# Gating w_in on the first batch's strided queries, one head of band v ahead of all, a w_out quarter moved forward and a new plan, in a fused sparse-attention and feed-forward kernel

## The chip, the cores and the metric

One core of one Trainium2 chip. The metric is the device time of one execution in microseconds (us), as the median of several runs. Most executions of one kernel lie within 0.3 to 1% of each other. Beside each experiment the kernel before was run again on the same chip. A ratio is the mean time of one kernel's fast runs over the mean of the other's fast runs of the same rounds, with a 95% interval, so it is not quite the ratio of the medians that are quoted.

## The reference

Eight batches of eight heads, 576 tokens, head size 64. Heads 0 to 3 ("local") see the last 32 positions, heads 4 to 7 ("strided") every 32nd. The result is laid out as 4608 tokens of 512 and goes through a feed-forward layer.

```python
rel = pos[:, None] - pos[None, :]
mask_local   = (rel >= 0) & (rel < 32)
mask_strided = (rel >= 0) & (pos[None, :] % 32 == pos[:, None] % 32)
attn = softmax(where(mask, q @ k.T / sqrt(64), -1e9)) @ v
x = attn.transpose(0, 2, 1, 3).reshape(4608, 512)
h = relu(x @ w_in)               # w_in  512 x 2048
out = (s * h * h + b) @ w_out    # w_out 2048 x 512
```

## The kernel before

The program is not written in the order in which it runs. A small planner, `Plan`, holds a clock `t` for TensorE, a time `free` for each other engine, and for each piece of work the time at which the plan believes it done. It puts out TensorE's steps one by one, and each posted job goes to the engine that the plan believes to be free first. The result is one fixed order for each engine, and each engine works through its own list in order. If the plan's times are wrong, nothing computes wrongly, as semaphores guard the data, but an engine stands at a job whose data are not there while later jobs could run.

```python
class Plan:
    LAT = {"A": 70.0, "V": 70.0, "P": 70.0, "D": 9000.0, "X": 9000.0}   # ns until a result counts as there
    ...
    def flush(self):
        ...  # of the posted jobs that are ready, the one ready first
            eng = min(p[1], key=lambda e: max(self.free[e], r) + p[1][e])
            end = max(self.free[eng], r) + p[1][eng]
            self.free[eng] = end
            p[2](eng)                       # emits the instructions, on that engine
            for k in p[3]:
                self.done[k] = end + self.LAT[eng]
...
def landing(cost):                          # when the plan believes a load to land
    nonlocal ring
    ring = max(ring, plan.t + 2000.0) + cost
    return ring + (6000.0 if plan.t > 60000.0 else 0.0)
```

("A" is ScalarE, "V" VectorE, "P" GpSimd, "D" a DMA transpose of q or k, "X" a DMA transpose of x, both issued by SyncE.) From batch 4 on, k comes transposed by DMA, and so does q. q is then spread into a block form by a copy that may go to three engines:

```python
plan.post([("in", "k" + sfx, b, mm), ("s", (b - back, m), 2)], {"D": 1300.0}, k_dma, [("k", id_)])
...
plan.post([("qT", id_), ("s", (b - 1, m), 2)], {"P": 2000.0, "V": 940.0, "A": 1340.0}, q_spread, [("q", id_)])
```

All loads from DRAM in the steady state are issued by GpSimd. The fetch of batch b+2 is held back twice: by the plan, which posts it when k of batch b+1 counts as transposed, and on the chip by a one-element "gate" copy that reads the transposed k.

```python
def fetch_qk(b):
    for mm in range(2):
        if (b - 1, "kTs", mm) in loaded:
            nc.gpsimd.tensor_copy(out=gate[0:1, 2 + mm:3 + mm], in_=loaded[b - 1, "kTs", mm][0:1, 0, 0:1])
    load_qk(b)
    ...
plan.post([...] + [("q", (b, mk)) for mk in range(4)] + [("k", (b, mk)) for mk in range(4)] +
          [("k", (b + 1 if b > 1 else b, mk)) for mk in range(2, 4)],
          {"P": 0.0}, lambda eng, b=b: fetch_qk(b + 2), [("fetch", b + 2)])
```

The start: w_in waits, by such a gate, for band v (v of the local heads, staged in w_out's buffer), and w_out comes after q, k of the second batch.

```python
def weights_in(eng):
    nc.gpsimd.tensor_copy(out=gate[0:64, 2:4].bitcast(FP32), in_=vl_stage[64:128, 0, 0, 0:1])
    load_w_in(True)
...
def second(eng):
    fetch_qk(1)
    weights_out(range(4))
    load_vl(1)
```

The softmax here doesn't subtract the row's maximum and nothing guards it: scores larger than these inputs give would overflow.

## Time and profile before

| | before |
|---|---|
| time, median of 5 runs beside the changed kernel | 321.53 us (319.93 to 321.97) |
| span of the profiled run | 321.0 us (this run took 322.85 us, more than all five) |
| TensorE busy | 309.6 us, 96% |
| granted TensorE clock, mean | 0.997 |

TensorE is the bound almost everywhere, so the busy share says little. The document uses a ledger as the prediction does: **lag** is a time minus the TensorE work done until then, work being the count of matmuls by their back-to-back intervals. A lag that stays constant over a stretch says that nothing was lost in it. The lags from here on were taken from all traces by one program, whose sum of work is 298.0 us, 1.0 below the sum that the prediction made by hand, so they are to be compared with each other and not to a tenth with those of the prediction. Waits that the text gives without a view are counted in the same way, from start to start less the work, and come out 0.2 to 0.3 us longer than the idle time in brackets. In the kernel before: 16.8 us at the second batch's first weighted sum (51.7 us), 19.4 at batch 3's (97.2 us, after the stall at 88 to 92 us that the prediction shows), 18.9 at the end.

### The profile page before, as it was taken

How to read it: one execution, taken by the hardware profiler on the slowest of the kernel's cores; microseconds unless marked ns; L12 is line 12 of the kernel's file. 1: busy time of each engine (PE TensorE's matmuls, PEld its weight loads, DVE VectorE, ACT ScalarE, POOL GpSimd, SP SyncE). 2: the span in 40 equal slices, each digit the busy share in tenths (PEclk: the TensorE clock that was granted, in tenths of full speed). 3: DMA queues.
4: the chain of work that ended last, by engine and by line, in shares of the span. 5: the costliest groups of instructions: out<-in, count | busy, mean ns of one | idle time of the engine just before them, and what ended most of it. 6: DMA issues, size and time to landing. Idle time of an engine off the chain costs nothing.

```text
span 321.0 us, 5972 instructions
## 1 busy us (share of the span) xinstructions
PE 309.6 (96%) x2184; PEld 173.1 (54%) x2184; DVE 193.9 (60%) x539; ACT 160.7 (50%) x301; POOL 106.0 (33%) x151
## 2 busy tenths in 40 slices
PE   8987899999989999999999999999999999999994
PEld 3763555666646555555655465545654445544441
DVE  6665864788888779655877377745874124443211
ACT  3774953398855575057753363555652026643100
POOL 7291628840793039700972078300000000000000
PEclk9999999999999999999999999999999999999998
DMA  8999999999989869999999899997204310000121
GB/s 118 181 144 205 212 181 159 189 211 94 95 92 164 135 112 167 151 166 170 132 134 132 163 160 158 140 159 173 73 18 70 102 48 33 2 33 34 43 91 65
DMA packets 110944, 39.41 MB, mean 123 GB/s; under 512 B 94706, under 2 KB 104562, under 8 KB 110914
## 3 DMA queue, kind: packets, MB, share of 16 engines
q0 software_dynamic: 65776, 18.66, 66.2%
q1 hardware_dynamic: 45138, 20.37, 32.5%
q8 instruction: 17, 0.28, 0.4%
q14 instruction: 13, 0.11, 0.1%
HBM read 38.15 MB, written 10.91 MB: 153 GB/s over the span
## 4 chain that ended last, share of the span: by engine, by line
PE 83%; DMA 8%; ACT 4%; POOL 2%; issue 2%; DVE 1%; SPq 0%; POOLq 0%; ACTq 0%
PE ps_f L683 38%; PE ps_f L648 34%; DMA ql<-in_q_dram 5%; PE ps_a L542 4%; PE ps_s L490 4%; DMA w_out_sb<-in_v_dram 2%; PE ps_t L374 1%; PE ps_a L706 1%; ACT pt L504 1%; ACT qD_loc L303 1%; POOL w_in L290 1%; POOL v_loc L303 1%; PE ps_f L542 0%; ACT u L666 0%; DVE gT L672 0%
## 5 line engine op out<-in xcount | busy, mean ns | idle before, releaser
L683 PE MATMUL ps_f<-w_out_sb,gT 128*128 128x512 f16 x576 | 145.4, 379 | 1.3 <-DVE gT L672 1.3
L666 ACT ACTIVATE u<-ps_f 128x512 f16<-128x512 f32 x136 | 80.9, 597 | 89.1 <-PE ps_f L648 69.9
L648 PE MATMUL ps_f<-xT,w_in_sb 128*128 128x512 f16 x432 | 108.7, 379 | 2.1 <-DMA w_in_sb<-in_moe_w_in_dram 2.1
L672 DVE TENSOR_TENSOR gT<-u 128x512 f16<-128x512 f16 x144 | 59.7, 419 | 44.2 <-ACT u L666 43.3
L683 PEld LDWEIGHTS <-gT 128*128 128x128 f16 x576 | 54.5, 98 | 55.4 <-DVE gT L672 1.7
L648 PEld LDWEIGHTS <-w_in_sb 128*128 128x128 f16 x432 | 45.7, 114 | 36.3 <-DMA w_in_sb<-in_moe_w_in_dram 2.6
L504 ACT ACTIVATE pt<-ps_s 128x384 f16<-128x384 f32 (+2 forms) x96 | 43.7, 489 | 21.1 <-PE ps_s L490 20.1
L694 DVE SCALAR_TENSOR_TENSOR o<-ps_f,s_sb,bcs 128x512 f32<-128x512 f32 x36 | 26.9, 746 | 33.0 <-PE ps_f L683 32.8
L542 PEld LDWEIGHTS <-pt 72*72 72x72 f16 (+1 forms) x448 | 32.1, 119 | 17.2 <-issue 0.8
L568 DVE TENSOR_TENSOR x_nat<-ps_a,rec 72x256 f16<-72x256 f32 (+1 forms) x76 | 35.0, 461 | 1.7 <-DVE rec L557 0.3
L648 PE MATMUL ps_f<-xT,w_in 128*128 128x512 f16 x136 | 35.3, 379 | 0.1
L557 DVE RECIPROCAL rec<-ps_a 72x4 f32<-72x4 f32 (+1 forms) x76 | 13.8, 181 | 18.4 <-PE ps_a L542 18.0
L277 POOL DMA_DIRECT2D v_loc<-in_v_dram x28 | 24.2, 879 | 1.8 <-issue 0.6
L648 PEld LDWEIGHTS <-w_in 128*128 128x128 f16 x144 | 14.9, 114 | 9.9
L282 POOL DMA_DIRECT2D v_str<-in_v_dram x16 | 13.1, 819 | 11.9 <-PE ps_a L542 6.5
L738 POOL COPY gate<-kT 1x1 f16<-1x1 f16 x6 | 1.2, 194 | 47.4 <-DMA kT<-ks 47.4
L512 DVE TENSOR_TENSOR pt<-pt,mask_loc 128x384 f16<-128x384 f16 x42 | 14.1, 352 | 3.5 <-ACT pt L504 2.7
L542 PE MATMUL ps_a<-v_str,pt 72*72 72x65 f16 x204 | 15.3, 197 | 0.0
L512 DVE TENSOR_TENSOR pt<-pt,mask_str 72x432 f16<-72x432 f16 (+1 forms) x42 | 14.3, 348 | 1.6 <-ACT pt L504 1.0
L542 PE MATMUL ps_a<-v_loc,pt 128*96 128x65 f16 x150 | 12.3, 206 | 0.0
L252 POOL DMA_DIRECT2D ql<-in_q_dram x16 | 11.9, 754 | 0.9 <-issue 0.9
L490 PE MATMUL ps_s<-qD_loc,kT_loc 128*128 128x192 f16 x72 | 11.1, 246 | 0.6 <-ACT pt L504 0.3
(104 smaller groups left out, 251.4 us busy)
## 6 DMA issues: line engine op xcount, KB each, us to landing
out_dram<-o SPq DMA_DIRECT2D x36, 256.0 KB, 3.6
v_loc<-in_v_dram POOLq DMA_DIRECT2D x28, 80.0 KB, 9.6
w_out_sb<-in_moe_w_out_dram POOLq DMA_DIRECT2D x4, 512.0 KB, 12.4
qs<-in_q_dram POOLq DMA_DIRECT2D x6, 288.0 KB, 6.2
ks<-in_k_dram POOLq DMA_DIRECT2D x6, 288.0 KB, 7.8
x_dram<-x_nat SPq DMA_DIRECT2D x10, 144.0 KB
ql<-in_q_dram POOLq DMA_DIRECT2D x4, 288.0 KB, 7.2
kl<-in_k_dram POOLq DMA_DIRECT2D x4, 288.0 KB, 8.4
```

Of the source, the lines that this page charges most:

```text
L277: nc.gpsimd.dma_start(out=vl[:, h, 1:LT, 0:D], in_=rest[:, h])
L490: nc.tensor.matmul(out=st["s", g][0:nk, c:c + 2 * nq], lhsT=(st["k"][:, i * nq:i * nq + nk] if loc else st["k"][:, i, 0:SQ]), rhs=st["q"][ ...
L504: nc.scalar.activation(out=pt[0:nk, 0:2 * n].rearrange("k t c -> k (t c)"), in_=st["s", g][0:nk, 0:2 * n * nq], func=AF.Exp, scale=scale)
L512: nc.vector.tensor_tensor(out=pt[0:nk, 0:2 * n], in0=pt[0:nk, 0:2 * n], in1=mask, op=ALU.mult)
L542: nc.tensor.matmul(out=st["a"][0:nq, j % per, :], lhsT=st["pt", g][0:nk, i, :], rhs=vt[0:nk, 2 * mm + e, j, :])
L557: nc.vector.reciprocal(out=st["rec", e, j][0:nq, 0:per], in_=st["pa", e, j][0:nq, 0:per, D:D + 1])
L568: nc.vector.tensor_tensor(out=st["x"][:, j0:j0 + per, 64 * e:64 * e + 64], in0=st["pa", e, j][0:nq, 0:per, 0:D], in1=st["rec", e, j][0:nq, ...
L648: nc.tensor.matmul(out=gts["h", T, ft], lhsT=(w_in_sb[min(ft // 4, 2) - 1][:, ct, :] if ft > 3 else w_in0[ct]).rearrange("p (c x l) -> p c ...
L666: nc.scalar.activation(out=gts["u", T, ft], in_=gts["h", T, ft], func=AF.Relu)
L672: nc.vector.tensor_tensor(out=gts[T][:, ft, :], in0=u, in1=u, op=ALU.mult)
L683: nc.tensor.matmul(out=gts["o", T, ts], lhsT=gts[T][:, ft, ts * 128:(ts + 1) * 128], rhs=w_out_sb[:, ft, :], start=(ft == 0), stop=(ft == ...
L694: nc.vector.scalar_tensor_tensor(out=o, in0=gts["o", T, ts], scalar=s_sb[:, 0:1], in1=bcs, op0=ALU.mult, op1=ALU.add)
```

## The change

The intent is to shorten the start. w_in's loads wait for the strided queries of batch 0, which land earlier than band v, one head of band v is loaded ahead of everything, and a quarter of w_out goes ahead of the second batch's q. Local q and k of batch 0 are transposed head by head straight from the load. The plan's constants are then fitted anew, among them which batches use DMA transposes. Three of the new constants belong to the steady state: loads after 60 us count as landed 4 us late instead of 6, x transposes take 10 us instead of 9, and a new key, "soon", lets the plan post a fetch 3 us after k's transposes are queued rather than 9 us after, when they count as done.

```diff
-    LAT = {"A": 70.0, "V": 70.0, "P": 70.0, "D": 9000.0, "X": 9000.0}
+    LAT = {"A": 70.0, "V": 70.0, "P": 70.0, "D": 9000.0, "X": 10000.0}
...
-                self.done[k] = end + self.LAT[eng]
+                soon = isinstance(k, tuple) and k[0] == "soon"
+                self.done[k] = end + (3000.0 if soon else self.LAT[eng])
...
-    KB_DMA, QS_DMA, XS_DMA = 4, 4, 3
+    KB_DMA, QS_DMA, XS_DMA = 3, 3, 4
...
     nc.sync.dma_start(out=ident, in_=h_ident.ap())
+    stage_v(range(1))
...
-                      k_dma, [("k", id_)])
+                      k_dma, [("k", id_), ("soon", id_)])
...
-        return ring + (6000.0 if plan.t > 60000.0 else 0.0)
+        return ring + (4000.0 if plan.t > 60000.0 else 0.0)
...
+    nc.gpsimd.tensor_copy(out=gate[0:8, 2:3], in_=loaded[0, "qs"][64:SQ, 0:1])
+    load_w_in()
+    ring = 14400.0
...
     def second(eng):
+        weights_out(range(1))
         fetch_qk(1)
-        weights_out(range(4))
+        weights_out(range(1, 4))
...
-                        [("k", (b + 1 if b > 1 else b, mk)) for mk in range(2, 4)],
+                        [("soon" if b > 1 else "k", (b + 1 if b > 1 else b, mk)) for mk in range(2, 4)],
```

Cut here: w_in in three pieces instead of six, band v loaded head by head with its 32 overlapping rows copied on chip (`rows_before`, on ScalarE, VectorE or GpSimd), the head-by-head transposes of batch 0, and other planned costs and arrival times.

## The prediction

> **What bounds the kernel now.** I read the page first, then the chain of waits, the timeline of TensorE, and the landing times of single transfers. The busy row says TensorE, and the slices say that it is full everywhere but at the start:
>
> ```profile
> PE 309.6 (96%) x2184; PEld 173.1 (54%) x2184; DVE 193.9 (60%) x539; ACT 160.7 (50%) x301; POOL 106.0 (33%) x151
> PE   8987899999989999999999999999999999999994
> ```
>
> 96% flatters it: the first slices hold filler matmuls on a tile of ones (26 in the first 10 us), and a matmul's busy time covers its latency. So I used a ledger. Start-to-start intervals of back-to-back matmuls, off the timeline, are 0.216 us for a 512-column one, 0.042 and 0.032 for a transpose of 96 and 72 columns, 0.082 and 0.063 for a score, some 0.045 and 0.035 for a weighted sum over v. All matmuls of the program without the fillers, in these intervals, make 299.0 us. The last matmul ends at 317.0 us, so 18 us are filler and waiting; the last 4.0 us are an eviction and the last transfer. The **lag** (time minus work done) tells where the 18 us arose:
>
> - at 25.2 us (first 16 matmuls of the first projection, 512 columns each, done): work 12.9, lag 12.3
> - at 33.2 us (first transpose of the second batch's q): work 18.3, lag 14.9
> - at 51.7 us (second batch's first weighted sum): work 35.2, lag 16.5
> - at 65.5 us (third batch's): work 49.0, lag 16.5
> - at the end: lag 18.0
>
> From 51.7 us on only 1.5 us are lost, so what the change can win lies almost all in the first 50 us. There the chain that ended last shows a string of transfers:
>
> ```profile
> 1.27 4.38 DMA ql<-in_q_dram
> 5.67 0.73 SPq L772
> 6.45 7.25 DMA w_out_sb<-in_v_dram
> 14.30 1.33 POOL w_in L290 x3
> ...
> 18.38 0.72 POOL w_in_sb L292
> 19.10 0.72 POOL w_in_sb L293
> 19.82 12.51 DMA ql<-in_q_dram
> 32.35 0.84 ACT qp L303
> 33.24 0.44 PE ps_t L374 x6
> ```
>
> Columns: start, length, what. q of batch 0 lands, band v is staged (in the buffer that w_out fills later) until 13.7 us, only then GpSimd issues w_in, and second-batch q queues behind it until 32.3. The cost on TensorE, from its timeline:
>
> ```profile
> 25.21 3.62 PE L648 MATMUL ps_f<-xT,w_in_sb 128*128 128x512 f16 x16
> 30.97 2.13 PE L648 MATMUL ps_f<-xT,w_in_sb 128*128 128x512 f16 x9 [2.14 <-DMA w_in_sb<-in_moe_w_in_dram]
> 33.24 0.43 PE L374 MATMUL ps_t<-ident,qp 96*128 96x96 f16 x6
> ```
>
> A wait of 2.14 us for the last piece of w_in, then second-batch q. The landings: vs of batch 0 at 13.4, w_in at 18.1 to 20.7 (first quarter, four pieces), 24.8 and 30.9, then ql 32.3, kl 33.8, qs 35.7, ks 37.1, w_out 39.2, 41.7, 44.8, 46.7, band v 50.9. From 13.4 to about 15.8 us the software queue moves nothing: that hole is what the gate costs.
>
> **What the Trainium skill says.** "TensorE: Matmul & The Clock Gate", Back-to-back issue gap: a lone warm matmul takes N/2.4 + 2.5 ns, 215.8 ns for 512 columns, and N/1.2 cold. The trace agrees: 216 ns, and 0.427 us for each of the first fillers. "DMA: Bandwidth & Descriptors", Queues, rings and completion order: each DMA engine goes round robin between queues, a packet of descriptors at a time. The trace agrees only in part: the SyncE band-v loads were issued from 6.45 us, yet none of their packets starts before 10.5 us, when the software queue thins out. "SBUF — State Buffer", SBUF: two separate sides: VectorE and GpSimd share a port pair as an exclusive lock. The trace fits it: four VectorE casts of v, 0.90 us together at 13.5 us, take 2.58 us beside a GpSimd memset, and TensorE loses about 1.4 us there (0.97 us of it is in the row below):
>
> ```profile
> 88.01 2.58 DVE L303 COPY v_str<-vs 72x512 f16<-72x512 f16 x4
> 88.21 1.83 POOL L264 MEMSET qs<- 16x2048 f16 x1
> 91.25 0.39 PE L683 MATMUL ps_f<-w_out_sb,gT 128*128 128x512 f16 x1 [0.97 <-DVE gT L672]
> ```
>
> **The change, part by part.**
>
> Gate of w_in. It now hangs on the eight last rows of qs, issued at 3.40:
>
> ```profile
> L270 POOL DMA_DIRECT2D qs<-in_q_dram x2: 606/628/651, 2.8 to 3.4; - x2
> DMA to landing us min/median/max: 6.3/6.5/6.6
> ```
>
> 3.40 + 6.33 = 9.73 us, against 13.70 for v: 4.0 us earlier. Descriptors take 0.7 us an issue, so w_in stands behind ks and vs before they are through, and the hole is filled. The pieces took about 2.5, 4.1 and 6.1 us one after the other; with band v beside them I expect about 17.5, 20.5 and 26. The first 16 projections end by about 25, the next 16 take 3.46 us more (28.4), so the last piece is there in time and the **2.14 us wait goes**.
>
> Band v. One head (147 KB) goes ahead of everything, when the queues are empty. The 32 overlapping rows are copied on chip, so a batch needs 2304 descriptors instead of 2944. Cost: small copies on ACT, VectorE and GpSimd, all off the path, and a memset six times as long on VectorE (0.27 to about 1.6 us, done before q lands). Ql may land a few tenths later than 5.65.
>
> Batch 0's local q and k are transposed head by head. In the program's order this is 48 transposes for 24, the pairing copies (0.62 us VectorE, 0.82 GpSimd/ACT) gone. The 24 extra cost 24 × 0.042 = 1.0 us, in a stretch where TensorE ran fillers.
>
> Batch 3 moves to DMA transposes. 24 local transposes leave TensorE; the 16 strided q ones leave and 16 of x come back. Sum: **−1.0 us in the stage where TensorE is full**. The work total stays at 299.0: a microsecond has moved from the full stage into the idle one.
>
> w_out's first quarter ahead of second-batch q. It puts some 2.4 us of transfer (the step from 39.2 to 41.7) before ql, which lands at about 26 + 2.4 + 1.4 = 29.8 instead of 32.3, 2.5 us earlier, not 4 to 5. In the new order TensorE does 36 matmuls of the projection before that transpose (41 before). By work it gets there at 25 + 20 × 0.216 = 29.3, and ql plus 0.4 us of pairing gives 30.2: a **new wait of 0.5 to 1 us**.
>
> Sum by the ledger. First 16 projections: work 13.9 (1.0 of transposes more). Work plus filler up to that point is 18.7 us in both orders, so I do not expect it much earlier: 24.8 for 25.2, lag 10.9 (before 12.3). Second-batch q: +0.7, lag 11.6 (14.9). Its evictions and scores lost 1.6 us until 51.7; I take 1.4, lag 13.0 (16.5). The rest lost 1.5 us; with new DMA timings I take the same 1.5, and 14.5 (18.0). Gain 3.5 to 4: span 321.0 − 3.7 = 317.3, measured time 0.8 longer as before, about **318 us**.
>
> **The rivals.**
>
> Starved band v. Heads 1 to 3 now compete with a software queue that does not run dry. If 256-byte packets only trickle, as between 6.5 and 10.5 us, ScalarE stands still: it casts head 1 after the second exp, in order, with four exps behind it. Landing at 13 instead of 11 us would push batch 0's attention back 1 to 2 us and halve the gain: 319.5 to 321. For: the 4 us delay in this trace. Against: the packets did run while ks and vs were finishing, and one head is already out of the way.
>
> The wait only moves. If w_out's quarter holds ql until 31 or later, the 2.14 us wait comes back under another name: 319 to 320. For: transfers are back to back to 52 us, so a shift of 4 us is all the queue can give. Against: w_out's quarter gives TensorE four bias matmuls to run early.
>
> Lost or found later. Batch 3 through 256-byte loads and DMA transposes can come late for a fixed TensorE order: +1 to +2 us, 319.5. Or the new order separates memset and cast and the 1.4 us at 88 to 92 us vanish: 316.5.
>
> Early attention. Were local attention to run ahead by its full 4 us, the projections would begin near 23 and the time near 315.5. Against: strided ks (11.2) and vs (13.4) are not earlier, and they gate the last quarter of x.
>
> **Range and chances.** Faster by over 2% needs 315.4 or less, a gain of 6.4 us: more than a third of all 18 us of filler and waiting, or both lucky rivals at once. Slower by over 2% would take 6.4 us of new waits, though TensorE has other work almost everywhere. I put 12% on faster, 86% on within 2%, 2% on slower; 315.3 to 320.5 should hold 8 times in 10.
>
> **What would show each step.** Right: w_in's first issue near 10 us, its last piece by 26 us and no wait of TensorE for it; second-batch q transposed near 30; lag 12.5 to 13.5 at the second batch's first weighted sum; 24 transposes fewer in batch 3. Wrong: ScalarE idle before its copy of v head 1; TensorE idle before the pairing of second-batch q by over 1 us; first projections after 25.5 us; the lag growing by over 2.5 us after 52 us. A lag under 9.5 at the first 16 projections would make the prediction too cautious.

## The result and the profile after

The changed kernel takes **340.34 us** (median of 5, 336.95 to 342.03) against 321.53 us: ratio 1.0559, 95% interval 1.0485 to 1.0632. It is slower by 5 to 6%, and the prediction was wrong in sign. The first rows of its page (busy time of the engines; TensorE's share and its granted clock in 40 slices of 8.4 us, in tenths):

```profile
PE 313.1 (93%) x2177; PEld 174.2 (52%) x2177; DVE 193.5 (58%) x543; ACT 157.4 (47%) x296; POOL 103.1 (31%) x150
PE   8799999999999919999979985999999999999995
PEclk9989999999999978999999997999999999999998
```

The start is whole, and a hole stands in slice 15 (118 us), with smaller ones in slices 21 and 24 to 25. The lag at the first local weighted sum of each batch says the same:

| first weighted sum of | before: time, lag | after: time, lag |
|---|---|---|
| batch 1 | 51.7, 16.8 | 46.7, 14.7 |
| batch 2 | 65.5, 17.0 | 64.3, 14.7 |
| batch 3 | 97.2, 19.4 | 94.7, 14.8 |
| batch 4 | 118.9, 19.3 | 118.5, 16.2 |
| batch 5 | 153.0, 19.2 | 149.2, 24.7 |
| batch 6 | 186.9, 19.1 | 177.4, 27.5 |
| batch 7 | 221.1, 19.0 | 211.9, 33.8 |
| last matmul | 316.8, 18.9 | 331.6, 33.6 |

Two cautions. First, the ledger counts the 48 small transposes of batch 0 in the changed kernel at 0.042 us each, 2.0 us. The trace shows that they run in pairs: the two of a pair of q start 3 ns apart and the pairs 0.042 us, so the 24 of q start within 0.50 us (from 6.96 us on), where the 12 of q in the kernel before start within 0.47 us (from 6.31 us on). So the changed kernel's work is 297.0 us, and 1.0 us more of its time than its column says is waiting. The difference of the two columns is still the lead, since what is left to do is counted alike, but 1.0 us of that lead is work that has left batch 3 and not time won at the start.

Second, traces of one start differ among themselves. The changed kernel and experiments 1, 3 to 6, 9, 13 and 14 give every engine the same instructions in the same order up to 50 us, and their lags lie between 12.6 and 16.2 us at the sixteenth projection and between 13.6 and 16.8 at batch 1. The four traces with the old start (before, experiments 2, 7 and 16) lie between 12.3 and 13.1, and between 14.8 and 16.8. So a difference of 1 or 2 us at the start between two single traces shows nothing by itself. With the 1.0 us added, the means at batch 1 are 15.5 us for the new start and 15.7 for the old.

By 97 us the change is 4.6 us ahead. Between there and 212 us it loses 19 us, and nothing after. Of the 18.9 us lost between 95 and 215 us, 15.5 are waits of over half a microsecond, 2.9 are 15 projection matmuls at half clock just after such waits, and 0.5 is small change. TensorE's timeline at the largest wait (start, length, engine, line, operation, count, and in brackets the idle time and what ended it), and its two costliest waits of the list:

```profile
125.82 0.88 PE L505 MATMUL ps_s<-qD_str,kT 128*72 128x144 f16 x6 [6.88 <-POOL qD_str L293]
126.49 1.91 PE L698 MATMUL ps_f<-w_out_sb,gT 128*128 128x512 f16 x4
```

```profile
PE ps_s L505 <- POOL qD_str L293: 6.9, 1, 6.9
PE ps_a L557 <- DVE x_nat L583: 4.8, 3, 3.5
```

The last line of the timeline shows the clock: four matmuls of 512 columns in 1.91 us, so 0.43 us from start to start instead of 0.216. The Trainium skill ("TensorE: Matmul & The Clock Gate", Part 1: The HAM clock gate) says that TensorE falls to half clock after an idle window of about 3.4 us; here the matmuls after a wait of 6.9 us ran at half clock, and the window from 118 to 128 us had a granted clock of 0.71 where the same window of experiment 3, which has no such wait, has 1.00. So a wait on TensorE costs more than its length.

What TensorE waited for from 118.8 us on is a copy of strided q on GpSimd. GpSimd's timeline shows why it came late:

```profile
116.34 0.18 POOL L753 COPY gate<-kT 1x1 f16<-1x1 f16 x1 [13.39 <-DMA kT<-ks]
117.09 2.95 POOL L248 DMA_DIRECT2D ql<-in_q_dram  x4
120.00 2.93 POOL L248 DMA_DIRECT2D kl<-in_k_dram  x4
122.86 0.80 POOL L266 DMA_DIRECT2D qs<-in_q_dram  x1
123.59 0.78 POOL L266 DMA_DIRECT2D ks<-in_k_dram  x1
124.31 1.46 POOL L293 COPY qD_str<-qT 64x576 f16<-64x576 f16 x2
```

GpSimd stood 13.4 us at the gate, then wrote ten loads in 7.2 us, and only then reached the copy, although the transposes of q that the copy reads had been queued on SyncE at 103.5 us, ahead of those of k (109.7) that the gate waited for. The waits at 200 and 207 us are of another kind: VectorE stands before a copy whose load is not there, and the small divisions (x_nat) that TensorE needs are behind it.

```profile
202.29 0.62 DVE L293 COPY qD_loc<-qTl 64x576 f16<-64x576 f16 x2 [4.70 <-DMA qTl<-ql]
207.48 0.33 DVE L293 COPY v_loc<-v_loc 32x640 f16<-32x640 f16 x1 [2.88 <-DMA v_loc<-in_v_dram]
```

Both kinds have one form: an engine that works in order stands at a job that the plan had expected to be ready.

### The profile page after: what moved, and what is told of

Its sections match the earlier page's. It is cut to its first block, busy times and chain, and to the rows that moved or that the text cites. A ratio compares the mean times of both kernels' runs of the same rounds, so it can differ in the third digit from the quotient of the medians.

```text
span 335.8 us, 5977 instructions
## 1 busy us (share of the span) xinstructions
PE 313.1 (93%) x2177; PEld 174.2 (52%) x2177; DVE 193.5 (58%) x543; ACT 157.4 (47%) x296; POOL 103.1 (31%) x150
## 4 chain that ended last, share of the span: by engine, by line
PE 76%; DMA 14%; POOL 4%; ACT 2%; issue 2%; DVE 1%; SPq 0%; POOLq 0%; DVEq 0%
PE ps_f L698 34%; PE ps_f L663 30%; DMA v_loc<-in_v_dram 5%; PE ps_s L505 4%; PE ps_a L557 3%; DMA ql<-in_q_dram 3%; DMA kT<-ks 3%; DMA kT_alt<-kl 2%; DMA w_out_sb<-in_v_dram 2%; POOL ql L248 1%; POOL kl L248 1%; PE ps_t L388 1%; PE ps_f L557 1%; PE ps_a L721 1%; ACT u L681 1%
## 5 line engine op out<-in xcount | busy, mean ns | idle before, releaser
L663 PE MATMUL ps_f<-xT,w_in_sb 128*128 128x512 f16 x568 | 150.2, 381 | 0.9 <-ACT u L681 0.5
L698 PE MATMUL ps_f<-w_out_sb,gT 128*128 128x512 f16 x576 | 148.6, 383 | 0.0
L681 ACT ACTIVATE u<-ps_f 128x512 f16<-128x512 f32 x139 | 82.1, 596 | 87.3 <-PE ps_f L663 69.5
L663 PEld LDWEIGHTS <-w_in_sb 128*128 128x128 f16 x576 | 61.9, 114 | 45.8 <-issue 2.2
L709 DVE SCALAR_TENSOR_TENSOR o<-ps_f,s_sb,bcs 128x512 f32<-128x512 f32 x36 | 26.9, 746 | 31.2 <-PE ps_f L698 31.1
L557 PEld LDWEIGHTS <-pt 72*72 72x72 f16 (+1 forms) x448 | 31.3, 120 | 21.0 <-issue 5.8
L271 POOL DMA_DIRECT2D v_loc<-in_v_dram x28 | 20.7, 755 | 2.7 <-DVE qp L293 1.3
L557 PE MATMUL ps_a<-v_str,pt 72*72 72x65 f16 x204 | 15.3, 197 | 4.9 <-DVE x_nat L583 4.8
L276 POOL DMA_DIRECT2D v_str<-in_v_dram x16 | 13.0, 816 | 13.8 <-PE ps_a L557 7.6
L505 PE MATMUL ps_s<-qD_str,kT 128*72 128x144 f16 x80 | 9.4, 236 | 7.1 <-POOL qD_str L293 6.9
L248 POOL DMA_DIRECT2D ql<-in_q_dram x20 | 14.7, 747 | 1.6 <-DMA ks<-in_k_dram 0.6
L293 ACT COPY qD_loc<-qTl 64x576 f16<-64x576 f16 x10 | 6.7, 670 | 17.7 <-DMA qTl<-ql 17.6
L527 DVE TENSOR_TENSOR pt<-pt,mask_str 72x432 f16<-72x432 f16 (+1 forms) x42 | 13.8, 344 | 2.1 <-ACT pt L519 1.8
L248 POOL DMA_DIRECT2D kl<-in_k_dram x20 | 14.6, 752 | 1.0 <-DVE rec L572 0.6
L505 PEld LDWEIGHTS <-kT 128*72 128x72 f16 x80 | 7.1, 119 | 10.2 <-issue 7.5
## 6 DMA issues: line engine op xcount, KB each, us to landing
w_out_sb<-in_moe_w_out_dram POOLq DMA_DIRECT2D x4, 512.0 KB, 10.9
v_loc<-in_v_dram POOLq DMA_DIRECT2D x28, 72.0 KB, 10.9
v_str<-in_v_dram POOLq DMA_DIRECT2D x16, 72.0 KB, 12.5
```

Of the source, the lines that this page charges most:

```text
L248: nc.gpsimd.dma_start(out=dst[:, h // 2, h % 2], in_=src[b, h].rearrange("(t p) d -> p t d", p=LQ))
L271: nc.gpsimd.dma_start(out=vl[LPAD:128, h, :, 0:D], in_=v_band(b, h))
L505: nc.tensor.matmul(out=st["s", g][0:nk, c:c + 2 * nq], lhsT=(st["k"][:, i * nq:i * nq + nk] if loc else st["k"][:, i, 0:SQ]), rhs=st["q"][ ...
L527: nc.vector.tensor_tensor(out=pt[0:nk, 0:2 * n], in0=pt[0:nk, 0:2 * n], in1=mask, op=ALU.mult)
L557: nc.tensor.matmul(out=st["a"][0:nq, j % per, :], lhsT=st["pt", g][0:nk, i, :], rhs=vt[0:nk, 2 * mm + e, j, :])
L663: nc.tensor.matmul(out=gts["h", T, ft], lhsT=w_in_sb[min(ft // 4, 2)][:, ct].rearrange("p (c x l) -> p c l x", x=128, l=4)[:, max(ft // 4 ...
```

## What the plan believed and what the chip did

The planner is deterministic, so the times it believed can be printed without a chip. The table sets the planned times of the fetches of batches 4 to 7 beside the first load of each fetch in the trace.

| kernel | planned fetches, us | apart | on the chip | apart |
|---|---|---|---|---|
| before | 88.9, 123.1, 157.1, 191.2 | 34.2, 34.0, 34.1 | 82.4, 117.8, 153.4, 187.1 | 35.4, 35.6, 33.7 |
| after | 81.2, 109.2, 136.4, 162.4 | 28.0, 27.2, 26.0 | 83.4, 117.1, 147.3, 182.1 | 33.7, 30.2, 34.8 |

The plan before was 3.7 to 6.5 us later than the chip, with time in hand. The new plan starts 2 us too early and runs at 26 to 28 us a batch, which the chip doesn't follow: by the last fetch it is 20 us off. The planned end of the last matmul is 311.4 us, the real one 331.7.

**Theory A (pace).** The plan's distance from fetch to fetch is a sum: load, allowance for late landing, DMA transposes, release. The change cuts two of its terms, 6 to 4 and 9 to 3, so 15 becomes 7, and the distance falls from 34 to some 27 us. On the chip the same loop takes over 30 us, so from batch 4 on each engine's list is laid for data that come later every time.

**Theory B (GpSimd order).** With the earlier release, fetches are laid ahead of copies on GpSimd, and the plan counts the fetch as 0 us while it stands at its gate and then takes 7 to 13 us. Copies behind it are late. The pace as such is harmless.

**Theory C (start or routes).** The start, or batch 3's DMA transposes, cause the late waits.

## The experiments

Sixteen kernels ran, and all gave correct results. The kernel before ran at a median of 321.53, 321.05, 320.93 and 320.76 us.

The expectations use the letters otherwise than this text. In those of experiments 1 to 4, "Theory A" is the copy behind the fetch on GpSimd (B here), "Rival B" is batch 3's transfers, and "Rival C" is the start. In those of experiments 5 to 7, "A2" is the plan's too early times (A here), and "Theory A alone" in experiment 5 is still the copy. Experiment 13 uses A and B as here; the "Theory A" of experiment 11 is its own.

### 1. Undo everything late, keep the start

The changed kernel with the old routes (4, 4, 3), 9 us for x, 6 us of allowance, and the release on landing:

```diff
-    KB_DMA, QS_DMA, XS_DMA = 3, 3, 4
+    KB_DMA, QS_DMA, XS_DMA = 4, 4, 3
-"X": 10000.0}
+"X": 9000.0}
-ring + (4000.0 if
+ring + (6000.0 if
-[("soon" if b > 1 else "k", ...)]
+[("k", ...)]
```

> The changed kernel with batch 3 on TensorE's transposes and the planner's late constants as before (fetch held until the planner counts k as landed, 6 us and 9 us for transfers); start as changed. Theory A and rival B both: the late waits go and the start's gain stays: 316 to 318. Rival C (the start itself, or the on-chip copy of the 32 rows in every batch, is what costs): 325 or more.

Measured: **321.29 us** (320.95 to 321.62), ratio 0.9998 (0.9966 to 1.0031). The lag is 14.3 us at batch 1, 14.9 at batch 3, 16.6 at the end: the 19 us are not lost. So the late part holds the loss, and theory C falls as far as the start goes. But the time is no better than before, and over the 316 to 318 expected. The ledger makes this run's work 299.0 us; with the pairs counted as they run it is 298.0, that of the kernel before, and the lags to set beside 16.8, 19.4 and 18.9 are 15.3, 15.9 and 17.6, with 1.7 us lost late. Since this is the whole changed start with the old late part, its ratio is the price of the start: no gain is shown, and one of over some 1.1 us is outside the interval, for the start together with the order that the plan then lays.

### 2. The late part alone

The kernel before, with those late changes and nothing of the start (diff as in 1, reversed, with the "soon" key).

> The kernel before with only the late part of the change: batch 3 by DMA transposes, the planner's late constants, the early release of the fetches. The spread of strided q of one pair again stands on GpSimd. Theory A: a stall of several us behind the fetch, 326 to 340. Rival C: within 2 us of before.

Measured: **343.58 us** (340.62 to 345.09), ratio 1.0681 (1.0617 to 1.0744); lag 14.8 at batch 1, 16.0 at batch 3, 40.4 at the end. The late part alone is enough, and the time is even above the 326 to 340 expected. At batch 3, before the loss, this kernel with the old start has a lag of 16.0, and the changed kernel has 15.8 with the 1.0 us added: up to there the traces show no difference that the start makes.

### 3. One line back: release on landing

```diff
-                        [("soon" if b > 1 else "k", (b + 1 if b > 1 else b, mk)) for mk in range(2, 4)],
+                        [("k", (b + 1 if b > 1 else b, mk)) for mk in range(2, 4)],
```

> The changed kernel with one line back: the fetch of a batch is released in the plan when k is counted as landed, not 3 us after its transposes are queued. Then no copy stands behind the waiting copies on GpSimd. Theory A: 316 to 322. Rival B: the waits for loads and transposes of the late batches stay, 328 or more.

Measured: **318.29 us** (317.43 to 319.07), ratio 0.9913 (0.9870 to 0.9956). Lag 13.8 at batch 1, 13.9 at batch 3, 13.4 at the end; no wait after 95 us. Planned fetches are 32 us apart (87.2, 119.2, 151.3, 183.4), and the chip's 31.2 to 31.9. TensorE's rows of the page, now without holes (slices of 7.9 us):

```profile
PE   7799999999999999999999999999999999999994
PEclk9989999999999999999999999999999999999999
```

One line holds the whole loss. The routes, the 10 us for x and the 4 us of allowance are not harmful by themselves. It is worth noting that the plan's own end is the same with and without the early release, 311.4 us: in the plan TensorE is full either way, and the early release bought nothing even there.

### 4. One copy moved off GpSimd

The changed kernel, with the one copy that TensorE waited for at 118.8 us put on VectorE and everything else in place:

```diff
-                copy_on(eng, out=st["q"][hs, :, e, :], ...)
+                copy_on("V" if id_ == (4, 3) else eng, out=st["q"][hs, :, e, :], ...)
```

> The changed kernel with one pair of copies (the spread of strided q of batch 4, second pair) on VectorE in place of GpSimd; every other instruction in the same place. Theory A (the copy stands on GpSimd behind two copies that wait for the transposes of k and behind ten loads, and TensorE stood 6.9 us for it): the wait near 119 us goes, some 8 us are won at the least, 332 or less. If the waits near 173 and 200 us are its after-effects (loads issued later, transposes later), the time falls to 317 to 322. Rival B (batch 3's transfers are too much for the DMA queues): no more than 8 us are won and the waits near 173 and 200 us stay: 331 to 333.

Measured: **340.8 us** median (334.04 in the profiled run, then 340.49, 341.1, 342.71); no ratio was formed, since three of the four runs lie over 1.5% above the first and count as slow. The wait at 118.8 us is gone from the trace, and others have come at 139.5, 140.7, 168.8, 197.6 and 201.9 us, up to 2.7 us each. In this one run 12 us are lost after batch 3 (lag 17.8 to 29.9) instead of 19, so about what the wait had cost was won; the other three runs are no shorter than the changed kernel's. The 332 us or less expected of the copy was not reached. What the copy alone is worth stays unclear, and with it gone at least 12 us of the loss are still there: the largest wait of the page is not the whole cause.

### 5. No copy of q on GpSimd

```diff
-{"P": 2000.0, "V": 940.0, "A": 1340.0}, q_spread,
+{"V": 940.0, "A": 1340.0}, q_spread,
```

> The changed kernel with GpSimd forbidden for the spreads of q, arrivals as optimistic as changed. Theory A2: the 7 us wait behind GpSimd goes, waits for late loads and transposes stay: 326 to 337. Theory A alone (only the copy behind the fetch): 316 to 321.

Measured: **334.51 us** (332.96 to 338.11), ratio 1.0401 (1.0340 to 1.0463). About 6 us of the loss go, 13 stay over the kernel before. Planned fetches are 26 to 28 us apart as in the changed kernel. The longest waits that remain come from landings: VectorE stood 13.5 us, four times, before copies of band v. This speaks against B as the whole.

### 6. The early release kept, later landings planned

```diff
-ring + (4000.0 if
+ring + (10000.0 if
```

> The changed kernel with the early release of the fetches kept, but the planner counting 10 us in place of 4 us on top of each late load (before: 6 us and the late release). Theory A2 (what hurts is that the plan counts on the late loads some 6 us before the chip has them, so that in-order engines stand before work that is not there): the late waits go, 316 to 320, like the run with the late release. Rival D (releasing the fetch early is bad by itself, through GpSimd's order or the queues): 328 or more.

Measured: **318.76 us** (317.84 to 319.39), ratio 0.9925 (0.9882 to 0.9967); lag 14.6 at batch 1, 14.3 at the end. Planned fetches: 81.2, 113.2, 145.3, 177.4, 32 us apart. The early release does no harm if another term of the sum restores the distance. This is what A says: 10 + 3 us are as good as 4 + 9.

### 7. The early release alone

The kernel before with the "soon" key and nothing else.

> The kernel before with only the early release of the fetches. Its plan had fetches 4 to 6 us later than the chip did; the early release takes about 6 us from that. Theory A2: the slack is gone, waits come, 323 to 333. Rival (the early release hurts only together with batch 3 by DMA): within 1% of before.

Measured: **354.48 us** (351.92 to 356.00), ratio 1.1024 (1.0947 to 1.1100). The direction was right and the size was not: I had said 323 to 333. Planned fetches are 28 to 30 us apart. GpSimd's timeline at the largest wait (17.6 us of TensorE, from 184.05):

```profile
183.66 0.40 POOL L739 COPY gate<-kT 1x1 f16<-1x1 f16 x1 [0.55 <-DMA kT<-ks]
184.24 2.93 POOL L253 DMA_DIRECT2D ql<-in_q_dram  x4 [0.19 <-issue]
198.80 1.61 POOL L283 DMA_DIRECT2D v_str<-in_v_dram  x2 [1.58 <-DMA v_loc<-in_v_dram]
200.40 1.40 POOL L304 COPY qD_str<-qT 64x576 f16<-64x576 f16 x2
```

From the gate to the copy 16 us pass: here the plan had laid both the fetch of q, k and that of v, 19 issues, ahead of the copy. So B exists as well, and I had left its size out.

### 8. Does ScalarE wait for band v at the start?

The version of experiment 3 with band v's casts not allowed on ScalarE:

```diff
-{"P": 1000.0, "A": 1000.0, "V": 900.0} if loc
+{"P": 1000.0, "V": 900.0} if loc
```

> The changed kernel with the late release of the fetches, and ScalarE forbidden for the casts of band v, so that it does not stand with four exps behind head 1 of v. If that wait set the start: first projections some 1.5 us earlier, 316 to 317.5 (318.3 without). If strided ks and vs set it: within 0.5 us of 318.3.

Measured: **320.74 us** (318.97 to 322.63), ratio 0.9989 (0.9930 to 1.0049). The lag at the sixteenth projection is 12.0 us instead of 13.3. It lies below all nine traces of the unchanged start (12.6 to 16.2, mean 13.9), so the prediction's rival "starved band v" is likely real, but one trace does not settle its size. And the plan came out anew, and 3 to 4 us are lost at 86 to 97 us to late evictions. No net gain.

### 9. A dose: 6 us instead of 3

```diff
-self.done[k] = end + (3000.0 if soon else self.LAT[eng])
+self.done[k] = end + (6000.0 if soon else self.LAT[eng])
```

> The changed kernel with the early release planned 6 us after the queueing of k's DMA transposes, not 3 us (9 us where they count as landed). The plan's fetches then stand at 84.2, 114.3, 143.4 and 172.5 us: 30.1, 29.1 and 29.1 us apart, against 28.0, 27.2 and 26.0 us in the changed kernel and some 32 us in the version with the release on landing. Theory 'the plan paces a batch faster than gate, loads and transposes go on the chip (31 to 32 us)': the shortage is 2 to 3 us a batch in place of 4 to 6, so less than half of the loss is left: 322 to 331 us, with TensorE's waits still behind transposes and strided q, in the second half. Rival 'any release before landing breaks the order': 336 or more. Rival 'a threshold: what the plan's 3 us cannot cover, 6 can': 318 to 320.

Measured: **339.82 us** (338.84 to 340.31), ratio 1.0589 (1.0549 to 1.0630). None of the expectations for A held; half the loss should have gone. The trace says what happened: one wait of 15.2 us at 118.4 us, against 7.0 in the changed kernel counted in the same way. TensorE's and GpSimd's timelines:

```profile
133.65 0.88 PE L505 MATMUL ps_s<-qD_str,kT 128*72 128x144 f16 x6 [15.02 <-POOL qD_str L293]
```

```profile
116.53 0.18 POOL L753 COPY gate<-kT 1x1 f16<-1x1 f16 x1 [15.52 <-DMA kT<-ks]
117.19 2.95 POOL L248 DMA_DIRECT2D ql<-in_q_dram  x4
127.31 2.43 POOL L276 DMA_DIRECT2D v_str<-in_v_dram  x3
132.20 1.39 POOL L293 COPY qD_str<-qT 64x576 f16<-64x576 f16 x2
```

With 6 us the plan posts the fetch of v 0.07 us after that of q and k, so both fetches stand before the copy. The fetch itself was only 3 us later than planned (114.3 and 117.2); what made 15 us of it is the 13 us of issuing that the plan counts as nothing. The dose test thus did not test the pace.

### 10 to 12. The parts of the start, on the version of experiment 3

```diff
gate_v:
-    nc.gpsimd.tensor_copy(out=gate[0:8, 2:3], in_=loaded[0, "qs"][64:SQ, 0:1])
+    nc.gpsimd.tensor_copy(out=gate[0:64, 2:4].bitcast(FP32), in_=vl_stage[64:128, 1, 0, 0:1])
-    ring = 14400.0
+    ring = 18000.0
w_out_after:
-        weights_out(range(1))
         fetch_qk(1)
-        weights_out(range(1, 4))
+        weights_out(range(4))
head_after:
-    stage_v(range(1))
...
-    stage_v(range(1, 4))
+    stage_v(range(4))
```

> The version with the release on landing (318.3 us), with w_in gated again on a landing of band v: its head 1 (the second of two transfers of v), in place of the strided queries of batch 0. Theory 'the gate is worth what w_in comes earlier': w_in is issued near 13.5 us instead of 10.3, its last piece lands some 3 us later (28 to 29), TensorE waits 1 to 3 us for it near 30 us, and the time is 319.5 to 321.5; band v heads 1 to 3 land earlier (by 11 us) because the software queue is not full, and ScalarE's wait for head 1 near 12 to 13 us goes. Rival 'the gate only trades w_in against band v': 317.5 to 319.

> The version with the release on landing (318.3 us), with all four quarters of w_out behind the second batch's q, k, qs, ks as in the kernel before. ql of the second batch should land near 27.3 instead of 29.7. Theory A, 'transfers are back to back, and TensorE has projections to do until 31 us in any case': no gain from the earlier q, and no second-layer matmuls early: 318 to 319.5. Rival, 'q of the second batch gates the whole of its attention': the lag at its first weighted sum falls by 1 to 2 us, 316.5 to 317.5.

> The version with the release on landing (318.3 us), with head 0 of band v no longer ahead of everything but with the other three behind the local queries' landing. Theory: ql of batch 0 lands 0.5 to 1 us earlier (near 6 instead of 6.9), but head 0 of v comes with the others at 11 to 13 us, head 1 some 0.5 us later, ScalarE and the first weighted sum wait for it: the lag at the first projections grows by 0.5 to 2 us, 318.5 to 320.5. Rival, 'the head ahead of all only delays q': 317 to 318.

Measured: gate_v **336.79 us** (336.70 to 336.94), ratio 1.0499 (1.0463 to 1.0535); w_out_after **320.45** (320.31 to 320.55), 0.9988 (0.9947 to 1.0029); head_after **318.57** (318.31 to 319.66), 0.9937 (0.9899 to 0.9975).

gate_v was a surprise. It has no early release, and its 18 us over experiment 3 are lost by the second batch's first weighted sum (lag 32.4 us against 13.8), 12.7 of them in one wait. TensorE and GpSimd:

```profile
53.25 0.66 PE L388 MATMUL ps_t<-ident,kp 96*128 96x96 f16 x6 [12.53 <-POOL kp L293]
```

```profile
41.44 0.68 POOL L251 DMA_DIRECT2D ql<-in_q_dram  x1 [2.17 <-issue]
48.66 2.94 POOL L271 DMA_DIRECT2D v_loc<-in_v_dram  x4
52.37 1.59 POOL L293 COPY kp<-kl 96x768 f16<-96x768 f16 x2
```

The later gate moved the plan, which then laid the pairing copy of the second batch's k (its load landed at 33.7 us) on GpSimd behind the fetches of that batch's v and of batch 2's q, k and v. This is cause B without any early release.

w_out_after: the second batch's q is transposed at 28.5 us instead of 31.3 in experiment 3, but the lag at batch 1 is 14.2, no better than 13.8, and some 2 us are lost between 60 and 97 us in the new order. That fits "no gain from an earlier q" (the first theory), with a larger loss than it gave. head_after: the interval overlaps that of experiment 3; whether one head ahead of all is worth anything stays unresolved.

### 13. The pace, with the fetch's cost told to the plan

The changed kernel, with GpSimd held by a fetch in the plan as well:

```diff
-{"P": 0.0}, lambda eng, b=b: fetch_qk(b + 2)
+{"P": 7000.0 if b > 1 else 0.0}, lambda eng, b=b: fetch_qk(b + 2)
-{"P": 0.0}, lambda eng: fetch_v(b + 2)
+{"P": 5500.0 if b > 1 else 0.0}, lambda eng: fetch_v(b + 2)
```

> The changed kernel (early release 3 us after queueing, fetches planned 26 to 28 us apart), with one thing more true in the plan: a fetch holds GpSimd for 7.0 us (q, k) and 5.5 us (v) where the plan counted 0. Planned fetch times stay (81.2, 109.2, 136.4, 162.6 us), but copies are no longer laid on GpSimd behind a fetch. Theory A, 'the pace of 26 to 28 us a batch is the loss': TensorE still waits for transposes and landings that come later than planned; near the kernel without GpSimd spreads (334.5): 328 to 336. Theory B, 'copies behind a fetch that waits are the loss': 318 to 321.

Measured: **339.06 us** (338.05 to 340.53), ratio 1.0567 (1.0523 to 1.0611). Planned fetches are those of the changed kernel to within 0.2 us. There is no copy behind a fetch any more, TensorE waits for no GpSimd, and the time is the same, 3 us above the upper end of A's range and far from B's 318 to 321. The lag grows from 15.0 at batch 3 to 35.1. So **the pace alone costs some 20 us** (18 over the kernel before, 21 over experiment 3). What TensorE waits for is now visible: copies of band v on VectorE that wait for landings, with the divisions behind them. TensorE at its largest waits, and VectorE ahead of the first:

```profile
143.13 0.40 PE L557 MATMUL ps_a<-v_str,pt 72*72 72x65 f16 x4 [5.61 <-DVE x_nat L583]
208.86 0.40 PE L557 MATMUL ps_a<-v_str,pt 72*72 72x65 f16 x4 [6.46 <-DVE x_nat L583]
```

```profile
139.25 0.33 DVE L293 COPY v_loc<-v_loc 32x640 f16<-32x640 f16 x1 [3.24 <-DMA v_loc<-in_v_dram]
```

The loop that sets the chip's pace is in SyncE's and GpSimd's timelines of this kernel. From the fetch on, the first at 117.40 us:

```profile
121.09 3.37 SPq L458 DMA_TRANSPOSE qTl<-ql  x2
127.20 2.94 SPq L440 DMA_TRANSPOSE kT_loc<-kl  x2
133.16 5.70 SPq L464 DMA_TRANSPOSE qT<-qs  x2
138.96 4.52 SPq L450 DMA_TRANSPOSE kT<-ks  x2
```

```profile
148.02 0.18 POOL L753 COPY gate<-kT 1x1 f16<-1x1 f16 x1 [13.35 <-DMA kT<-ks]
148.84 2.94 POOL L248 DMA_DIRECT2D ql<-in_q_dram  x4 [0.31 <-issue]
```

ks was issued at 123.9 and landed at 133.2 us, after the ten loads had gone through; then SyncE transposed strided q and strided k one behind the other until 143.5 us, the gate opened at 148.0, and the next fetch began at 148.84: 31.4 us for one turn. In the traces of the nine kernels with a plan of 26 to 30 us a turn (after, experiments 2, 4, 5, 7, 9, 13, 14, 16) no turn from batch 4 on was shorter than 30.2 us.

### 14. The dose again, without the second cause

Experiments 9 and 13 together: 6 us, and the fetch's cost told.

> As the last, with the release planned 6 us after queueing: fetches 29 to 30 us apart (84.2, 114.3, 143.4, 172.5). The kernel with 6 us and no cost of the fetch ran 339.8 us, and 15.2 of its 18 us lost after 95 us were one wait at 118.4 us, for strided-q copies laid on GpSimd behind two fetches. Theory 'two causes, and at this pace the second is nearly all': the wait is gone, and 1 to 5 us of waits for k's transposes and local q remain: 319 to 323. Rival 'the pace alone would have cost as much, the one wait only hid it': 330 or more.

Measured: **328.43 us** (326.46 to 330.83), ratio 1.0236 (1.0177 to 1.0295). The 15 us wait is gone, with 11 us gained on experiment 9. But 10 us are left over experiment 3, more than the 1 to 5 that I gave the pace of 29 to 30 us; the remaining waits are for k's transposes at 169.7 us (3.5) and for an activation at 173.8 (3.1).

### 15 and 16. The second cause taken out of experiments 10 and 7

gate_v with the second batch's pairing copies not allowed on GpSimd, and soon_alone with the strided q copies not allowed there:

```diff
gate_v_nop:
-**({"P": 900.0} if b in (1, 2, 3) else {})
+**({"P": 900.0} if b in (2, 3) else {})
soon_alone_nop:
-{"P": 2000.0, "V": 940.0, "A": 1340.0}, q_spread,
+{"V": 940.0, "A": 1340.0}, q_spread,
```

> The version with w_in gated on band v's head 1, with the pairing copies of the second batch not allowed on GpSimd. Without that the run stood at 336.8 us, with one TensorE wait of 12.7 us at 40.3 us for a pairing copy laid on GpSimd behind two fetches. Theory: the wait goes, and the rest is the price of the later w_in: w_in's last piece lands near 26.8, ql of the second batch near 31.5 as in the run before: 319.5 to 322. Rival, the gate costs nothing: 318 to 319.

> The kernel before with the early release alone (354.5 us), and the strided q spread not allowed on GpSimd. Fetches are planned at 82.9, 112.7, 140.7 and 168.7 us (28 to 30 us apart). Theory 'two causes': the 22 us of waits for spreads on GpSimd go, and what the pace costs stays, some 5 to 15 us over the kernel before: 326 to 336. Rival 'all GpSimd order': 319 to 323. Rival 'all pace': 345 or more.

Measured: gate_v_nop **320.56 us** (319.99 to 321.22), ratio 0.9988 (0.9952 to 1.0024): with the copy off GpSimd 16.2 us go, the wait of 12.7 us and what followed from it. What is left against experiment 3 is 0.75 points of ratio, some 2.4 us, within the expectation; the two intervals together allow 0.6 to 4. The lag at the sixteenth projection is 17.0 us against 13.3. So the later gate, with the plan that goes with it, costs some 2.4 us. soon_alone_nop **340.42 us** (340.22 to 342.11), ratio 1.0618 (1.0576 to 1.0659): GpSimd's order was 14 us of the 33, and the pace 20, more than the 5 to 15 that I had expected; the time lies in none of the three ranges set for it.

### All together

The plan's two terms, its distance between fetches, and the time. The last column says whether TensorE waited for over 5 us on a copy that GpSimd had behind a fetch.

| kernel | allowance + release, us | planned distance, us | time, us | copy behind a fetch |
|---|---|---|---|---|
| before | 6 + 9 | 34 | 321.5 | no |
| experiment 1 | 6 + 9 | 34 | 321.3 | no |
| experiment 3 | 4 + 9 | 32 | 318.3 | no |
| experiment 6 | 10 + 3 | 32 | 318.8 | no |
| experiment 14 | 4 + 6 | 29 to 30 | 328.4 | no |
| experiment 9 | 4 + 6 | 29 to 30 | 339.8 | yes |
| experiment 16 | 6 + 3 | 28 to 30 | 340.4 | no |
| experiment 7 | 6 + 3 | 28 to 30 | 354.5 | yes |
| after | 4 + 3 | 26 to 28 | 340.3 | yes |
| experiment 13 | 4 + 3 | 26 to 28 | 339.1 | no |
| experiment 5 | 4 + 3 | 26 to 28 | 334.5 | no |
| experiment 4 | 4 + 3 | 26 to 28 | 340.8 | no |
| experiment 2 | 4 + 3 | 26 to 27 | 343.6 | no |

Experiments 8, 10 to 12 and 15, planned 32 us apart, concern the start. At 32 us and more nothing is lost in the late part. Below, without a copy behind a fetch, the loss does not follow the distance evenly: 10 us in experiment 14 (29.4 us in the mean) and 16 to 21 in experiments 5 and 13 (27), all over experiment 3, but 20 in experiment 16 (28.6), over the kernel before. In the changed kernel the two causes are not additive: taking the second one out gives 0 (experiment 13) or 6 us (experiment 5), which fits that a wait for one late datum covers another. The loss can be read off the turns: in experiment 14 the plan's three from batch 4 on make 88 us (30.1, 29.0, 29.2) and the chip's 99.7 (33.8, 30.3, 35.6), 11 to 12 us more, for 10 us lost; in the changed kernel 81 and 98.7, some 17.5 more, with 2.2 at the first fetch, for 19 lost. Open is why the chip's turns come out longer under a short plan (30.2 to 36.1 us, once 42.1 in experiment 9) than in experiments 3 and 6 with a plan of 32 us (31.2 to 32.2): the stalls that a turn causes may lengthen the next one, but no run shows that by itself. Open is also the share of the two terms: experiments 3 and 6 show that either will do, not that they are the same thing to the chip.

Experiment 3 is the best version that ran: the change with one line back, 0.9913 of the kernel before.

## Why the prediction was wrong

The step that made it wrong in sign is the last term of its sum, "The rest lost 1.5 us; with new DMA timings I take the same 1.5": the rest lost 18.9 us, through the plan's pace. The steps in order:

- **First 16 projections at 24.8 us.** They ended at 27.9 in the changed kernel, lag 14.2 against 12.5 before by the same ledger, so not earlier but later, by 1.7 us in the ledger and by 2.7 us with the pairs of transposes counted as they run, over the 25.5 us that the prediction itself had set as a sign of error. The nine traces of this start lie at 26.3 to 29.9 us, the four of the old one at 25.0 to 25.8. TensorE waited 1.7 us at 13 us for an exp whose predecessor on ScalarE is the cast of band v's head 1, for which ScalarE had stood 2.1 us (another of the signs set), and q of batch 0 landed at 6.9 us instead of 5.7. This is the rival "starved band v", which experiment 8 makes likely (1.3 us less lag there in one trace).
- **w_in's pieces at 17.5, 20.5 and 26; ql at 29.8; the 2.14 us wait gone.** Right: 18.0, 20.5 and 25.4; ql at 29.6; no wait for w_in. The gate opened at 10.1 instead of 9.7. The new wait of 0.5 to 1 us before second-batch q did not come: TensorE reached that transpose late, at 32.2 us, with the data there. Experiment 15 prices the earlier gate at some 2.4 us, in the version without the early release.
- **Gain of 3.5 us at the second batch's first weighted sum.** This failed too. The ledger gives 2.1 us in the changed kernel's trace (16.8 to 14.7) and 3.0 in experiment 3, but 1.0 of each is the double count of the pairs, and the mean of nine traces with the new start against four with the old leaves 0.2 us (15.5 against 15.7, spread 2 to 3 us). Experiment 1 agrees: the new start with the old late part runs at 0.9998 of the kernel before. w_in does come earlier, but the first projections come later, and no net gain is shown. w_out's quarter is not shown to help through an earlier or later q (experiment 11).
- **The 1.4 us at 88 to 92 us.** I named the vanishing of this stall as a lucky rival, and it vanished: the lag does not grow between batch 1 and batch 3 (14.7, 14.8), where it grew by 2.5 us before.
- **"The 24 extra cost 24 × 0.042 = 1.0 us", and the work stays at 299.0.** Not so: they run in pairs, the 48 in the time of 24, so the work falls by 1.0 us.
- **"−1.0 us in the stage where TensorE is full."** It holds as far as the runs tell: experiment 1, with the old routes, has 1.0 us more work.
- **"The rest lost 1.5 us; with new DMA timings I take the same 1.5."** This is the step that failed. The rest lost 18.9 us. The rival "Lost or found later" named the place (DMA transposes late for a fixed TensorE order) and gave it 1 to 2 us and batch 3. The mechanism was of that kind, but its cause is the plan's pace from batch 4 on and its size was ten times what I gave. I read the changed constants as fine tuning of an order, and did not ask what they sum up to over a turn of the loop. The working was at hand: 6 + 9 us became 4 + 3, so the plan's turn of 34 us became 27, and the trace of the kernel before shows fetches 34 to 36 us apart with a gate that stood 15 us at each. The planner itself, which runs without a chip, would have printed 81.2, 109.2, 136.4 and 162.4 us.
- **Chances.** I gave 2% to slower by over 2%, with the reason that TensorE has other work almost everywhere. It has, but behind the stalled instruction in its fixed order, where it is of no use.

Experiment 3, which is the change without the early release, ran at 318.3 us, and the prediction was 318.0. That is luck. The prediction had its gain at the start, with the work unchanged. By experiment 1 the start gains nothing that is shown; of the 2.8 us that experiment 3 gains on the kernel before, 1.0 is work that left batch 3, which the prediction had cancelled against the transposes of batch 0, and the rest is of the size of the 2.5 us that the kernel before loses between batches 1 and 3 by this ledger, which the prediction had left in as part of its 1.5. No run takes this rest apart. The last addition, "0.8 longer as before", was misread as well: the span of 321.0 us belongs to a run of 322.85, so 1.85, and the sum would have come to some 319.2.

## What to carry to other kernels

When a program's order is fixed by assumed times, look at the assumed period of each loop, the sum of its latencies, and compare it with the period in the trace; here a plan 2 us a turn too slow lost under 2 us in all, and one 4 us too fast lost that at every turn and more, as the in-order engines stood together. Don't release work in a plan before the chip's own gate can open, and charge the issuing engine for what it issues. And do not mend the largest wait of a profile before asking whether many small ones share its cause: moving the copy behind the 6.9 us wait left the median where it was (340.8 us against 340.3), though one run of four was 6 us shorter.

## What the Trainium skill lacked or had wrong

- "DMA: Bandwidth & Descriptors", Issuing engines are not separate DMA queues, calls the time on the sequencer that starts a DMA usually small relative to the DMA itself. Here it was not: a quarter of ql (72 KB) held GpSimd for 0.75 us and landed 3.2 us after its issue (medians of the changed kernel), and two fetches back to back held it from 117.2 to 132.2 us in experiment 9, 1.7 us of it a wait. No page was found that says that a copy in order behind them waits for all of that.
- "DMA: Bandwidth & Descriptors", Anatomy of one DMA, gives 2.0 us + bytes / 436e3 for one DMA, an estimate of 2.2 us for 72 KB. In this queue a band-v load of 72 KB took 10.9 us in the median from issue to landing and one of ql 3.2. The fit is no basis for planned arrivals where loads queue.
- "Advanced Engine Details and Errata", X-Bar Transpose (TRN2), says that transposing DMAs are as fast as regular ones. It lacks what they cost the engine that issues them on this chip (another page has cycle counts, in a table on a path of trn3 alone): pairs of them held SyncE's queue for 2.9 to 5.7 us in experiment 13, one behind the other, and they were the second half of the 31.4 us turn.
- "DMA: Bandwidth & Descriptors", Queues, rings and completion order: the round robin between queues did not show at the start of the kernel before, where band v's packets, issued from 6.45 us, did not start before 10.5 us; why is not shown.
- "TensorE: Matmul & The Clock Gate" was right on the half clock (0.43 us each) after the 6.9 us wait. Back-to-back issue gap gives the 216 ns for 512 columns as the gap of an isolated matmul and about 131 ns for a sustained stream; here a stream ran at 216 ns too (84 in a row took 18.14 us from 298.86 us on in the kernel before).
